# Gated recurrence and highway FFN on one core: zero matmuls in every early wait of TensorE, the diagonal on GpSimd, and a new order of the work

## The chip, the core and the metric

The kernel runs on one core of a Trainium2 chip. TensorE (PE) multiplies matrices into PSUM, a memory of 8 banks; VectorE (DVE), ScalarE (ACT) and GpSimd (POOL) do the rest, and SyncE (SP) issues the loads and stores of the large arrays. The metric is the device time of one execution in microseconds.

## The reference

A recurrence along the sequence, one for each channel, feeds a highway layer. B = 4, S = 6336, D = 256, so the second part has 25344 tokens of 256 channels. All arrays are float32.

```python
sig = 1 / (1 + exp(-f_logit))
f = lower_bound + (1 - lower_bound) * sig
for t in range(S):                       # per batch and channel
    h = f[:, t] * h + (1 - f[:, t]) * x[:, t]
    y[:, t] = h
x = y.reshape(B * S, D)
H = relu(x @ w_h); T = sigmoid(x @ w_t + b_t)
out = T * H + (1 - T) * x
```

## The kernel before

The tokens go through in 22 units: 128, 128, 256 and 512 tokens, four units of 1024, seven double units of 2048 (two loads each), five of 1024, one of 512 and one of 256. Every array is kept channel by channel on the partitions after a transpose on TensorE, in two halves of 128 channels. With u = sigmoid(-f_logit) the kernel computes f = 1 - c*u (c = 1 - lower_bound), scans the product u*x with f into a scaled y, and gets d = max(-c*y, (w_h - I) y) and the gate t = sigmoid(w_t y + b_t) from it. The output is diag(c)*y + d*t, formed by two matmuls that transpose back and add in PSUM.

What runs when is written out by hand in a string, `order`, of one line of tokens after another. Each token calls one small function, and the instructions keep the order of the string on each engine. A token reads "letter, unit.half or unit.chunk.half, colon, place": after the colon stands the SBUF slot or, for work of TensorE, the PSUM bank. A `v` at the end picks the other engine. The letters that the change and the prediction name:

- `l`, `x`: load of f_logit and of x, issued by SP (L279); `wh`, `wt`: loads of the two weights.
- `u`: sigmoid on ACT (L291). `i`: transposes of u (PE, L320). `f`: decay, on ACT (L345) or with `v` on DVE (L343).
- `b`, `B`: half or whole product u*x (L307, L311), on POOL or with `v` on DVE. `p`: transposes of the product (PE, L351 for 128 tokens, L357 beyond). `s`: scan on DVE (L365), whose inputs are f and the transposed product in PSUM.
- `z`, `g`: matmuls of the FFN for the gate and for d (PE, L378 and L156). `t`: gate on ACT (L401). `d`: on DVE (L408). `e`, `E`: half or whole gated product d*t (L422), on POOL or with `v` on DVE.
- `o`: output matmuls (PE, L441 and L442), `c`: copy out of PSUM on ACT (L457) or with `v` on DVE (L455), `w`: store (SP, L464).
- `dg`: the two diagonal matrices diag(c), on POOL (L242) or with `v` on DVE (L240). `cb`: copy of the bias, on DVE or with `v` on ACT. `WI`: w_h - I (POOL, L248). `WH`, `WT`: weights times c (ACT). `pb`, `pc`, `cc`: transposes of the two constants, and c.
- `k*N:bank`: N matmuls of a block of zeros into the second half of a PSUM bank. Nobody reads what they write. The first of a token is recorded at L268, the others through the helper at L156, which long FFN matmuls use too.

The part of the string between the first load and the scan of unit 3 is the place that matters here. `p2.0.1:6 p2.0.0:1`, for example, are the two transposes of unit 2's product, into banks 6 and 1, and `s2.1` and `s2.0` are the scans that read them. The instructions of several engines are recorded one after another, and the tile framework puts a wait wherever a later one touches what an earlier one writes or reads. POOL's two-input operations get one more wait (`shared`): on the last such operation of DVE that was recorded ahead of them.

Of the kernel before, what the change touches and what calls it, by code (L numbers as in the profile page):

```python
# [61 lines left out]
g4.0.0:01 d4.0.0 x6.0:3 l7.0:4 u7.0:16 B6.0:15 p6.0.1:3 s6.1:17 x7.0:5 p6.0.0:6 z5.0.0:45 t5.0.0:19 z5.0.1:01
g5.0.1:45 l8.0:6 e4.0.1 u8.0:25 s6.0 t5.0.1 d5.0.1:9 g5.0.0:23 d5.0.0 l8.1:7 u8.1:14 i7.0.0:7 f7.0v:22 g6.0.0:01
i7.0.1:6 f7.1 e4.0.0 o4.0.1:45 c4.0.1:11 i8.1.1:23 i8.0.1 f8.1:18 x8.0:8 d6.0.0:23 B7.0:8 p7.0.1:6 p7.0.0:7 o4.0.0:45
c4.0.0:13 z6.0.1:01 t6.0.1:21 x8.1:9 s7.0:26 z6.0.0:23 t6.0.0 i8.0.0:45 i8.1.0 f8.0:24 l9.1:1 l9.0:0 g6.0.1:01 B8.0:28
s7.1 z7.0.0:23 t7.0.0:3 g7.0.1:67 B8.1:7 d6.0.1 u9.1:4 E5.0v E6.0 p8.0.1:45 z7.0.1:01 l10.1:2 x9.1:3 x9.0:4 d7.0.1:15
B9.1:6 p8.1.1 t7.0.1 o5.0.1:23 c5.0.1:12 s8.1:16 o5.0.0:67 c5.0.0:8 u9.0:5 p8.0.0:01 p8.1.0 o6.0.0:23 c6.0.0:27
o6.0.1:67 c6.0.1:25 s8.0:22 x10.1:6 u10.1:14 i9.0.0:45 i9.1.0 f9.0:19 l10.0:7 l11.0:5 g7.0.0:23 d7.0.0 B9.0:9
i9.1.1:67 i9.0.1 f9.1:20 x11.1:8 u10.0:28 g8.0.1:01 d8.0.1:7 B10.1:21 w6.0.1 x10.0:9 w2.0.0 g8.1.1:23 d8.1.1:18
p9.1.1:45 p9.0.1 s9.1:17 l11.1:1 E7.0 z8.0.1:01 z8.1.1:67 t8.1.1:23 t8.0.1:4 z8.0.0:23 t8.0.0 i10.1.1:67 i10.0.1  # L70
f10.1:24 p9.1.0:01 p9.0.0 l12.0:0 z8.1.0:23 t8.1.0 i10.1.0:45 w0.0.0 w1.0.0 x13.0:3 x11.0:2 l13.0:4 i10.0.0 f10.0:5
o7.0.0:67 c7.0.0:25 u11.1:6 s9.0:20 g8.1.0:23 u11.0:9 g8.0.0:01 d8.1.0 d8.0.0 g9.1.0:45 d9.1.0:10 z9.0.0:67 t9.0.0:14
l12.1:7 B10.0:3 e8.0.1 g9.1.1:23 d9.1.1 p10.1.0:01 p10.0.0 s10.0:19 z9.1.0:45 t9.1.0:2 o7.0.1:23 c7.0.1:28 E8.1
z9.1.1:67 t9.1.1 e8.0.0 i11.0.1:45 i11.1.1 f11.1:0 p10.0.1:23 p10.1.1 o8.1.1:67 c8.1.1:15 o8.1.0:01 c8.1.0:26 B11.1:23
s10.1:3 E9.1v o8.0.0:45 c8.0.0:21 g9.0.1:67 w4.0.0 o8.0.1:01 c8.0.1:5 x12.1:6 z9.0.1:45 t9.0.1 d9.0.1:4 g10.0.1:23
u12.1:18 w8.1.0 l13.1:9 w3.0.0 g9.0.0:01 d9.0.0 i11.1.0:45 d10.0.1:13 i11.0.0 f11.0:7 g10.1.1:67 d10.1.1:16 g10.0.0:01
d10.0.0 x12.0:1 w6.0.0 B11.0:22 o9.1.0:23 b12.1.0:24 u12.0:2 p11.1.0:45 c9.1.0:6 p11.0.0 s11.0:26 o9.1.1:67 c9.1.1:9
w9.1.1 z10.0.0:01 t10.0.0:1 E9.0 i12.1.1:23 i12.0.1 f12.1:10 z10.1.1:67 t10.1.1:27 p11.0.1:01 p11.1.1 s11.1:22
B12.0:23 o9.0.0:45 c9.0.0:14 o9.0.1:23 c9.0.1:7 z10.0.1:67 t10.0.1 g10.1.0:45 d10.1.0 b12.1.1 u13.1:9 i12.0.0:23
i12.1.0 f12.0:4 u13.0:17 g11.0.1:67 d11.0.1:20 x13.1:5 l14.0:8 w5.0.0 B13.1:2 g11.1.0:01 w8.1.1 w8.0.1 g11.1.1:45  # L80
d11.1.0:0 w8.0.0 d11.1.1 w9.1.0 z11.1.1:67 t11.1.1:18 g11.0.0:23 d11.0.0 z11.1.0:01 t11.1.0 p12.1.1:45 p12.0.1 E10.0v
E11.1 s12.1:8 z11.0.0:23 t11.0.0:15 l21.0:7 l14.1:2 x14.0:0 b13.0.0:5 e11.0.0 z10.1.0:67 z11.0.1:01 t10.1.0 l15.0:1
w9.0.0 x14.1:9 t11.0.1 i13.1.1:23 i13.0.1 f13.1:21 p12.1.0:67 p12.0.0 s12.0:1 o10.0.0:01 c10.0.0:6 o11.1.1:45
c11.1.1:24 w11.1.1 w4.0.1 l16.0:6 e11.0.1v e10.1.1v o10.0.1:23 c10.0.1:23 i13.0.0:01 i13.1.0 f13.0:18 w10.0.1
p13.1.0:45 o11.1.0:23 c11.1.0:10 g12.0.1:67 d12.0.1:13 g12.1.0:01 d12.1.0:9 u14.1:4 g12.0.0:23 d12.0.0 b13.0.1 e10.1.0
u14.0:0 b14.0.1:15 o11.0.0:67 p13.0.0 s13.0:14 c11.0.0:17 o11.0.1:01 c11.0.1:20 z12.0.0:23 t12.0.0:22 i14.1.0:67
i14.0.0 p13.1.1:01 p13.0.1 s13.1:26 f14.0:24 o10.1.0:23 c10.1.0:27 z12.0.1:45 t12.0.1 l17.0:4 B14.1:11 b14.0.0
z12.1.0:67 t12.1.0:2 i14.0.1:23 i14.1.1 f14.1:5 g12.1.1:45 d12.1.1 o10.1.1:67 c10.1.1v:18 g13.1.0:01 d13.1.0:23
l20.0:5 x15.0:2 z13.0.1:23 e12.1.0 g13.0.0:45 u15.0:4 g13.1.1:67 d13.0.0:21 t13.0.1:0 u16.0:3 x16.0:3 z12.1.1:01
t12.1.1 d13.1.1 p14.0.1:23 p14.1.1 s14.1:16 z13.1.1:45 t13.1.1:19 z13.1.0:67 t13.1.0 E12.0 o12.0.0:01 c12.0.0:22  # L90
z13.0.0:45 t13.0.0 p14.0.0:67 w11.0.0 w11.1.0 l18.0:8 w10.1.1 e12.1.1 p14.1.0 i16.0.1:0 f16.1:17 x17.0:9 x19.0:0
x18.0:1 B15.0:10 o12.1.0:12 c12.1.0:2 w12.1.0 w7.0.1 w9.0.1 s14.0:15 o12.1.1:34 c12.1.1:11 i16.0.0:5 i15.0.0:0 f15.0:5
o12.0.1:12 g13.0.1:34 d13.0.1 c12.0.1:18 E13.1 f16.0 u18.0:9 w10.0.0 g14.0.0:67 d14.0.0:1 i15.0.1:0 g14.1.0:12
d14.1.0:8 g14.1.1:34 d14.1.1 g14.0.1:67 d14.0.1 f15.1 p15.0.1:5 s15.1:13 E13.0 u17.0:24 z14.0.0:12 t14.0.0:4 p15.0.0:0
s15.0 z14.1.1:34 B16.0:19 t14.1.1:2 z14.0.1:67 t14.0.1 o13.1.1:12 c13.1.1:10 i17.0.1:3 E14.0v w5.0.1 z14.1.0:45
t14.1.0 w10.1.0 E14.1v b17.0.0:0 w11.0.1 o13.0.0:67 c13.0.0:28 o13.0.1:12 c13.0.1:7 i18.0.1:0 g15.0.0:45 f18.1:6
# [408 lines left out]
```

## Time and profile before

| | |
|---|---|
| median of 3 executions | 209.36 us (209.15 to 209.79) |
| the profiled execution, its own time | 211.39 us |
| its span in the trace | 209.6 us |
| mean granted TensorE clock | 0.995 |
| busy: PE, DVE, ACT, POOL | 191.9, 192.9, 192.7, 171.4 us |
| moved by DMA | 78.68 MB, mean 375 GB/s over the span |

A row of the timeline gives the start (us from the start of the span), the length from there to the end of the last instruction of the group, the engine, the line of the kernel, the operation, out<-in by the program's names, out<-in by shape and type, and the number of instructions. In brackets stands the idle time of the engine just before, and what ended it. A row of groups gives, behind the bar, the busy time in us and the mean of one instruction in ns, and then the idle time before them. A row by stages gives the stage's limits and length, the busy time and instructions of the engine asked for, the granted clock, and the share and rate of the DMA engines.

### The profile page before, as it was taken

The page shows a single profiled execution, that of the slowest core. Times are in us where ns is not written, and L with a number is a line of the kernel's source. Part 1 is how long each engine was busy: PE and PEld are TensorE (multiplying, and loading weights), DVE is VectorE, ACT ScalarE, POOL GpSimd, SP SyncE. Part 2 cuts the span into 40 slices and gives each one's busy share as a digit, 9 for nine tenths or more (in the row PEclk, how much of TensorE's full clock was granted, in tenths as well). Part 3 has the DMA queues.
Part 4 walks back from the last instruction along what each step waited for, and adds up shares of the span by engine and source line. Part 5 has one row for each costly group of instructions (what it writes and reads, how often), then busy time and mean ns, then how long its engine had stood idle before and what let it go on. Part 6 is the DMA issues. An engine that isn't in the chain of part 4 may idle for free.

```text
span 209.6 us, 4643 instructions
## 1 busy us (share of the span) xinstructions
PE 191.9 (92%) x1852; PEld 138.6 (66%) x1877; DVE 192.9 (92%) x138; ACT 192.7 (92%) x193; POOL 171.4 (82%) x72
## 2 busy tenths in 40 slices
PE   7898979799988889999899998999998999999991
PEld 3586846385774647958655967657856886677680
DVE  0667999999999899999999999999999999999981
ACT  4556999999999999999999999999998999998892
POOL 4502489998899999979997978997999599998940
PEclk9999999999999999999999999999999999999998
DMA  5999999999999999799999999999999999664976
GB/s 173 344 429 419 414 421 416 421 419 410 421 420 373 386 428 419 306 277 408 355 344 421 429 417 421 420 418 421 425 413 415 423 411 414 263 245 192 357 263 244
DMA packets 17133, 78.68 MB, mean 375 GB/s; under 512 B 1876, under 2 KB 3160, under 8 KB 11224
## 3 DMA queue, kind: packets, MB, share of 16 engines
q1 hardware_dynamic: 17104, 78.39, 93.7%
q8 instruction: 14, 0.23, 0.4%
q14 instruction: 7, 0.06, 0.1%
q10 hardware_dynamic: 8, 0.00, 0.0%
HBM read 52.43 MB, written 25.95 MB: 374 GB/s over the span
## 4 chain that ended last, share of the span: by engine, by line
PE 32%; ACT 19%; DVE 14%; issue 10%; DMA 5%; POOL 4%; ACTq 0%; DVEq 0%; POOLq 0%
DVE y L365 11%; PE psum L378 10%; ACT t L401 6%; PE psum L156 5%; PE psum L442 5%; PE psum L441 5%; ACT o L457 5%; DMA out_dram<-o 5%; ACT f L345 4%; ACT u L291 3%; PE psum L320 3%; PE psum L357 3%; POOL bv L311 2%; POOL d L422 2%; DVE d L408 2%
## 5 line engine op out<-in xcount | busy, mean ns | idle before, releaser
L365 DVE TENSOR_TENSOR_SCAN y<-f,y,psum 128x1024 bf16<-128x1024 f16 (+7 forms) x42 | 104.4, 2512 | 4.5 <-PE psum L357 3.7
L311 POOL TENSOR_TENSOR bv<-u,x 128x2048 bf16<-128x2048 f16 (+2 forms) x29 | 95.6, 3314 | 8.9 <-issue 3.9
L422 POOL TENSOR_TENSOR d<-d,t 128x1024 bf16<-128x1024 bf16 (+3 forms) x28 | 72.8, 2618 | 18.7 <-ACT t L401 11.1
L378 PE MATMUL psum<-y,w_sb 128*128 128x512 bf16 (+2 forms) x242 | 78.6, 363 | 4.6 <-DVE y L365 2.0
L408 DVE SCALAR_TENSOR_TENSOR d<-y,ncc,psum 128x1024 bf16<-128x1024 bf16 (+3 forms) x62 | 62.9, 1056 | 1.2 <-PE psum L156 0.5
L401 ACT ACTIVATE t<-psum,bt 128x1024 bf16<-128x1024 f32 (+3 forms) x62 | 57.9, 983 | 5.8 <-PE psum L378 2.2
L156 PE MATMUL psum<-y,w_sb 128*128 128x512 bf16 x149 | 56.4, 379 | 0.7 <-DVE y L365 0.6
L345 ACT ACTIVATE f<-psum,ncc 128x1024 f16<-128x1024 f16 (+4 forms) x40 | 52.1, 1323 | 2.6 <-PE psum L320 2.6
L291 ACT ACTIVATE u<-l 128x2048 f16<-128x2048 f32 (+3 forms) x29 | 49.3, 1720 | 2.1 <-DMA l<-in_f_logit_dram 2.1
L457 ACT COPY o<-psum 128x1024 f32<-128x1024 f32 (+2 forms) x55 | 48.5, 926 | 1.9 <-PE psum L442 1.8
L442 PE MATMUL psum<-ident_b,d 128*128 128x128 bf16 x396 | 48.7, 219 | 1.3 <-POOL d L422 1.1
L441 PE MATMUL psum<-diag,y 128*128 128x128 f16 x396 | 48.9, 219 | 0.2
L442 PEld LDWEIGHTS <-d 128*128 128x128 bf16 x396 | 43.5, 112 | 4.6 <-POOL d L422 1.9
L441 PEld LDWEIGHTS <-y 128*128 128x128 bf16 x396 | 43.6, 112 | 1.8
L378 PEld LDWEIGHTS <-w_sb 128*128 128x128 f16 x248 | 23.5, 99 | 20.3 <-DVE y L365 2.1
L320 PE MATMUL psum<-ident_h,u 128*128 128x128 f16 x396 | 29.3, 221 | 2.7 <-ACT t L401 1.7
L320 PEld LDWEIGHTS <-u 128*128 128x128 f16 x396 | 25.3, 99 | 8.4 <-issue 3.1
L357 PE MATMUL psum<-ident_f,bv 128*128 128x128 f32 x196 | 28.0, 276 | 0.7 <-POOL bv L311 0.7
L156 PEld LDWEIGHTS <-w_sb 128*128 128x128 f16 x168 | 16.4, 97 | 18.1 <-issue 3.7
L357 PEld LDWEIGHTS psum<-ident_f,bv 128*128 128x128 f32 x196 | 22.3, 142 | 5.8 <-POOL bv L311 1.7
L422 DVE TENSOR_TENSOR d<-d,t 128x2048 bf16<-128x2048 bf16 (+3 forms) x12 | 10.5, 891 | 0.4 <-ACT t L401 0.3
L156 PE MATMUL psum<-zeros 128*128 128x256 bf16 x55 | 9.8, 322 | 0.0
(36 smaller groups left out, 45.0 us busy)
## 6 DMA issues: line engine op xcount, KB each, us to landing
l<-in_f_logit_dram SPq DMA_DIRECT2D x23, 1024.0 KB, 15.9
x<-in_x_dram SPq DMA_DIRECT2D x23, 1024.0 KB, 15.9
out_dram<-o SPq DMA_DIRECT2D x43, 512.0 KB, 9.0
out_dram<-o SPq DMA_DIRECT2D x12, 256.0 KB, 2.4
l<-in_f_logit_dram SPq DMA_DIRECT2D x2, 512.0 KB, 10.1
...
```

Of the source, the lines that this page charges most:

```text
L156: return pe.add_instruction(mybir.InstMatmult(name=nc.get_next_instruction_name(), start_tensor_calc=start, stop_tensor_calc=stop, tile_si ...
L311: shared(pin(e.tensor_mul(st[n]["bv", s][:, a:c].rearrange("p k d j -> p k j d"), st[n]["u", s][:, 2 * a:2 * c].rearrange("p (k j) d -> p ...
L320: pin(nc.tensor.transpose(uT[:, j * P:(j + 1) * P], st[n]["u", s][:, j, h * P:(h + 1) * P], ident_h))
L345: pin(nc.scalar.activation(to, of, AF.Identity, scale=ncc[:, h:h + 1], bias=1.0))
L365: pin(nc.vector.tensor_tensor_scan(y[:, c:e], st[n]["f", h][:, c:e], data, 0.0 if fresh else carry[h], op0=ALU.mult, op1=ALU.add))
L378: pin(nc.tensor.matmul(p.part(a, e), w, data, start=ki == 0, stop=ki == NH - 1))
L401: pin(nc.scalar.activation(half(n, q, "t", m), z, AF.Sigmoid, bias=bt[:, m:m + 1]))
L408: pin(nc.vector.scalar_tensor_tensor(half(n, q, "d", m), y, ncc[:, m:m + 1], g, op0=ALU.mult, op1=ALU.max))
L422: shared(pin(e.tensor_mul(d, d, t)), not eng)
L441: pin(nc.tensor.matmul(o, st[n]["y", h][:, whole], diag[:, h], start=True, stop=False))
L442: pin(nc.tensor.matmul(o, half(n, q, "d", h)[:, cols], ident_b, start=False, stop=True))
L457: pin(nc.scalar.copy(to, op))
```

## The change

Only the string changes, in all its lines; the functions, the units, the shapes and the arithmetic stay.

- Zeros: 72 before the middle of the program instead of 65, in more and other places. Before, in order: 2, 4, 2, 12, 8, 4, 5 and 23 in bank 7, 3 in bank 5, 2 in bank 6. After: 1, 2, 4, 2, 1, 3, 14, 3, 2, 5, 1, 1, 1, 24 and 2 in bank 7, 6 in bank 6.
- `dgv` becomes `dg`: the diagonal moves from DVE to POOL, and later in the string. `cbv` becomes `cb`: the bias is copied by DVE instead of ACT.
- Decays: f0.1, f1.0, f1.1 and f2.0 go to DVE (f0.0 stays, f2.1 moves to ACT); f7.1 instead of f7.0 on DVE; f21.0 from DVE to ACT.
- Gated products: E0.0 and the second half of E2.0 move from DVE to POOL; E20.0 is whole on DVE instead of half; E18.0 instead of E19.0 is on DVE.
- First loads: x0, l0, l1, l2, x1, x2, wh, wt instead of l1, l0, x0, l2, x1, wh, x2, wt.
- PSUM banks: p2.0.1 and p2.0.0 go to banks 5 and 7 (6 and 1 before), p3.0.1 and p3.0.0 to 7 and 0 (3 and 1 before), g1.0.1 to 7 (6 before).
- The rest of the work stands in another order, with other slots and banks.

```diff
-i2.0.0:5 f2.0 p1.0.1:4 WI WH cbv x2.0:5 wt WT b2.0.0:10 k*12:7 p2.0.1:6 p2.0.0:1 g0.0.0:7 dgv s1.1 s2.1:11 s2.0
...
-B3.0v:20 z0.0.0:0 z2.0.0:4 t2.0.0 d2.0.0 e2.0.0 E1.0 t0.0.0 e2.0.1v k*5:7 p3.0.1:3 s3.1:21 l4.0:8 u4.0:22 p3.0.0:1
-s3.0 k*23:7 z3.0.0:5 t3.0.0:23 i4.0.1:2 f4.1:24 E0.0v x4.0:9 B4.0v:25 g3.0.0:6 z3.0.1:7 t3.0.1 d3.0.0:26 e3.0.0
...
+i2.0.1:4 f2.1:9 x2.0:5 b2.0.0:10 i2.0.0:1 f2.0v k*3:7 p2.0.1:5 p2.0.0:7 p1.0.1:4 wh WI s1.1 WH k*14:7 g1.0.0:6
+g0.0.0:0 g0.0.1:3 s2.0:11 wt WT k*3:7 z1.0.1:2 z0.0.1:1 s2.1 z1.0.0:4 g1.0.1:7 k*2:7 z2.0.1:5 d0.0.1:12 l3.0:6 u3.0:13
+z2.0.0:3 t1.0.1:14 t1.0.0 k*5:7 g2.0.0:2 k*1:7 i3.0.1:4 t2.0.0:15 t2.0.1 d1.0.0:16 t0.0.1:17 f3.1:18 g2.0.1:6 z0.0.0:3
+t0.0.0 k*1:7 i3.0.0:5 f3.0 dg d1.0.1 d0.0.0 x3.0:7 b3.0.1v:19 l4.0:8 u4.0:20 b3.0.0v k*1:7 p3.0.1:7 p3.0.0:0 E0.0
+d2.0.0:21 k*24:7 i4.0.1:1 f4.1:22 x4.0:9 d2.0.1 s3.1:23 E2.0 s3.0 z3.0.0:2 z3.0.1:4 B4.0v:24 g3.0.0:3 d3.0.0:25
...
```

In the built program the first place is TensorE around the transposes of unit 2's product (`bv_167` before, `bv_157` after; `psum_61` is all of PSUM; the scan reads what the L357 rows write). Before:

```order
L156 LDWEIGHTS zeros_62
L156 MATMUL psum_61<-zeros_62 128x256
L357 MATMUL psum_61<-ident_f_71,bv_167 128x128 [waits DVE_49,Pool_49]
L357 MATMUL psum_61<-ident_f_71,bv_167 128x128
L378 LDWEIGHTS w_sb_96 [waits Activation_49]
L378 MATMUL psum_61<-y_143,w_sb_96 128x128
```

After:

```order
L156 LDWEIGHTS zeros_62
L156 MATMUL psum_61<-zeros_62 128x256
L357 MATMUL psum_61<-ident_f_71,bv_157 128x128 [waits Pool_49]
L357 MATMUL psum_61<-ident_f_71,bv_157 128x128
L351 LDWEIGHTS bv_143
L351 MATMUL psum_61<-ident_b_76,bv_143 128x128 [waits Activation_49]
L268 LDWEIGHTS zeros_62
L268 MATMUL psum_61<-zeros_62 128x256
```

Before, the twelve zeros of `k*12:7` stand ahead of the transposes, and an FFN matmul follows them. Now three zeros stand ahead; behind the transposes come that of unit 1's second half (L351, which waits for ACT) and the fourteen zeros of `k*14:7`.

The second place is TensorE around the transposes of unit 3's product (`bv_253` and `bv_264`). Before:

```order
L156 LDWEIGHTS zeros_62
L156 MATMUL psum_61<-zeros_62 128x256
L357 MATMUL psum_61<-ident_f_71,bv_253 128x128 [waits DVE_49]
L357 MATMUL psum_61<-ident_f_71,bv_253 128x128 x3
L268 LDWEIGHTS zeros_62
L268 MATMUL psum_61<-zeros_62 128x256
```

After:

```order
L320 LDWEIGHTS u_219
L320 MATMUL psum_61<-ident_h_66,u_219 128x128
L268 LDWEIGHTS zeros_62
L268 MATMUL psum_61<-zeros_62 128x256 [waits DVE_49]
L357 MATMUL psum_61<-ident_f_71,bv_264 128x128 [waits DVE_49]
L357 MATMUL psum_61<-ident_f_71,bv_264 128x128 x3
L268 LDWEIGHTS zeros_62
L268 MATMUL psum_61<-zeros_62 128x256
```

A block of zeros follows the transposes in both (23 before, 24 now). Before, that block stands behind `s3.1` and `s3.0` in the string, and writes to bank 7, from which no scan of unit 3 reads; now it stands ahead of `s3.1` and writes to the bank of p3.0.1.

The third place is DVE from the scans of unit 2 (`y_188` before, `y_194` after) to those of unit 3 (`y_272`, `y_316`); `d_197`, `d_201`, `d_240` before and `d_215`, `d_241`, `d_277` after belong to units 0, 1 and 2. Before:

```order
L365 SCALAR_TENSOR_TENSOR y_188<-f_136,y_145,psum_61 128x256 [waits PE_49,Activation_49]
L408 SCALAR_TENSOR_TENSOR d_197<-y_143,ncc_93,psum_61 128x128 [waits PE_49]
L408 SCALAR_TENSOR_TENSOR d_201<-y_145,ncc_93,psum_61 128x128 [waits PE_49]
L408 SCALAR_TENSOR_TENSOR d_197<-y_143,ncc_93,psum_61 128x128 [waits PE_49]
L408 SCALAR_TENSOR_TENSOR d_201<-y_145,ncc_93,psum_61 128x128 [waits PE_49]
L408 SCALAR_TENSOR_TENSOR d_240<-y_188,ncc_93,psum_61 128x256 [waits DVE_49]
L311 TENSOR_TENSOR bv_253<-u_195,x_251 128x2x2x256 [waits DMAHW3_49,Activation_49]
L408 SCALAR_TENSOR_TENSOR d_240<-y_188,ncc_93,psum_61 128x256 [waits DVE_49,PE_49]
L422 TENSOR_TENSOR d_240<-d_240,t_224 128x256 [waits DVE_49,Activation_49]
L365 SCALAR_TENSOR_TENSOR y_272<-f_237,y_188,psum_61 128x512 [waits PE_49,Activation_49]
```

After:

```order
L365 SCALAR_TENSOR_TENSOR y_194<-f_153,y_148,psum_61 128x256 [waits DVE_49]
L408 SCALAR_TENSOR_TENSOR d_215<-y_135,ncc_93,psum_61 128x128 [waits PE_49]
L408 SCALAR_TENSOR_TENSOR d_241<-y_148,ncc_93,psum_61 128x128
L408 SCALAR_TENSOR_TENSOR d_241<-y_148,ncc_93,psum_61 128x128 [waits PE_49]
L408 SCALAR_TENSOR_TENSOR d_215<-y_135,ncc_93,psum_61 128x128
L311 TENSOR_TENSOR bv_264<-u_219,x_262 128x2x256 [waits DMAHW3_49,Activation_49]
L311 TENSOR_TENSOR bv_264<-u_219,x_262 128x2x256
L408 SCALAR_TENSOR_TENSOR d_277<-y_194,ncc_93,psum_61 128x256 [waits DVE_49,Activation_49]
L408 SCALAR_TENSOR_TENSOR d_277<-y_194,ncc_93,psum_61 128x256 [waits DVE_49]
L365 SCALAR_TENSOR_TENSOR y_316<-f_245,y_194,psum_61 128x512 [waits PE_49,Activation_49]
```

The product of unit 3 (L311) stands behind all four d of units 0 and 1 in both; its two halves are instructions of their own now, both d of unit 2 come behind them, and the half gated product (L422) has left DVE here.

More of the change, by code (lines that the diff above doesn't have):

```diff
@@ L62 @@
[L62 to L96, printed above, removed]
```

81 lines of the change are left out of this document (57 added, 24 removed).

## The prediction

> **What bounds the kernel now.** I read the page's busy shares first, then the busy time of the vector engine (DVE) by stages, then the first 30 us of each engine in order of time.
>
> ```profile
> span 209.6 us, 4643 instructions
> PE 191.9 (92%) x1852; PEld 138.6 (66%) x1877; DVE 192.9 (92%) x138; ACT 192.7 (92%) x193; POOL 171.4 (82%) x72
> ```
>
> Three engines are busy for 92% of the span, so the average does not say which one is late. The stages do (start:end, length, DVE busy and instructions, granted clock, DMA share, GB/s):
>
> ```profile
> 0.00:4.50 4.50, 0.27 (x1) 1.00 0.47 152
> 4.50:18.00 13.50, 8.23 (x20) 1.00 0.99 388
> 18.00:205.60 187.60, 184.43 (x117) 1.00 0.96 384
> 205.60:209.60 4.00, 0.00 (x0) 0.75 0.55 202
> ```
>
> From 18.0 to 205.6 us DVE rests for 187.60 - 184.43 = 3.17 us in all. Whatever moves the moment at which DVE starts to run without a break therefore moves the end, less what of these 3.17 us can be given back. That moment is the scan of unit 3, s3.1, at 18.01:
>
> ```profile
> 5.22 0.28 DVE L343 TENSOR_SCALAR f<-psum,ncc 128x128 f16<-128x128 f16 x1 [0.42 <-PE psum L156]
> 8.47 1.06 DVE L240 TENSOR_SCALAR diag<-ident_h,cc 128x128 f16<-128x128 f16 x2
> 9.46 0.47 DVE L365 TENSOR_TENSOR_SCAN y<-f,y,psum 128x128 bf16<-128x128 f16 x1
> 11.69 1.39 DVE L365 TENSOR_TENSOR_SCAN y<-f,y,psum 128x256 bf16<-128x256 f16 x2 [1.76 <-PE psum L357]
> 12.99 0.58 DVE L408 SCALAR_TENSOR_TENSOR d<-y,ncc,psum 128x128 bf16<-128x128 bf16 x2
> 13.75 0.35 DVE L408 SCALAR_TENSOR_TENSOR d<-y,ncc,psum 128x128 bf16<-128x128 bf16 x1 [0.18 <-PE psum L156]
> 14.31 0.74 DVE L408 SCALAR_TENSOR_TENSOR d<-y,ncc,psum 128x128 bf16<-128x128 bf16 x2 [0.20 <-PE psum L378]
> 14.96 1.30 DVE L311 TENSOR_TENSOR bv<-u,x 128x1024 bf16<-128x1024 f16 x1
> 16.15 0.48 DVE L408 SCALAR_TENSOR_TENSOR d<-y,ncc,psum 128x256 bf16<-128x256 bf16 x1
> 18.01 2.45 DVE L365 TENSOR_TENSOR_SCAN y<-f,y,psum 128x512 bf16<-128x512 f16 x2 [1.18 <-PE psum L357]
> 20.38 0.27 DVE L422 TENSOR_TENSOR d<-d,t 128x256 bf16<-128x256 bf16 x1
> 20.56 2.47 DVE L311 TENSOR_TENSOR bv<-u,x 128x2048 bf16<-128x2048 f16 x1
> ```
>
> The brackets tell what the old order loses: 1.76 us before s2 and 1.18 us before s3, both on TensorE's transposes of the products (L357). Two smaller brackets matter more for the new order. At 5.22 f0.0, and at 13.75 d0.0.0, wait for L156 as a zero matmul, an instruction whose result nobody reads. Here is TensorE at the same time:
>
> ```profile
> 8.88 2.55 PE L156 MATMUL psum<-zeros 128*128 128x256 bf16 x11
> 11.23 0.63 PE L357 MATMUL psum<-ident_f,bv 128*128 128x128 f32 x2
> 12.29 0.42 PE L268 MATMUL psum<-zeros 128*128 128x256 bf16 x1
> 12.51 1.21 PE L156 MATMUL psum<-zeros 128*128 128x256 bf16 x7
> 14.65 0.49 PE L156 MATMUL psum<-zeros 128*128 128x256 bf16 x3
> 16.98 0.27 PE L268 MATMUL psum<-zeros 128*128 128x256 bf16 x1 [0.95 <-ACT t L401]
> 17.52 0.60 PE L357 MATMUL psum<-ident_f,bv 128*128 128x128 f32 x4
> 18.07 2.13 PE L156 MATMUL psum<-zeros 128*128 128x256 bf16 x18
> ```
>
> The eight zeros of 12.29 and 12.51 end at 13.72, and d0.0.0 starts at 13.75. Its operand g0.0.0 lies in bank 7, whose other half those zeros write, and in the built program its wait counts up to the last of them. So a reader of a PSUM bank that stands behind a block of zeros of the same bank, in the order's text, waits for the whole block. At 16.98 the reverse is seen: the zeros of bank 7 wait 0.95 us for the reader t0.0.1.
>
> These rows also give the price of a zero. From the first start to the last it is (2.55 - 0.42)/10 = 0.213 us early on, and (2.13 - 0.27)/17 = 0.109 us later; the block at 12.51 is where the pace doubles.
>
> **The change, part by part.** The diagonal: the DVE row at 8.47 loses its 1.06 us. GpSimd does it now, in a gap that these rows show:
>
> ```profile
> 6.80 0.87 POOL L248 TENSOR_TENSOR w_raw<-w_raw,ident_f 128x128 f32<-128x128 f32 x2 [0.58 <-DMA w_raw<-in_moe_w_h_dram]
> 8.16 1.17 POOL L311 TENSOR_TENSOR bv<-u,x 128x512 bf16<-128x512 f16 x1 [0.49 <-DMA x<-in_x_dram]
> 17.37 1.30 POOL L422 TENSOR_TENSOR d<-d,t 128x256 bf16<-128x256 bf16 x2 [8.04 <-ACT t L401]
> ```
>
> The 8.04 us of idle hide it; without them it could cost what GpSimd needs for 128x128 of floats, 0.87/2 us each by its subtraction of the identity (the row at 6.80), 0.9 us. I take zero for GpSimd. On DVE the gain also counts nothing, since DVE has to wait for TensorE right behind it.
>
> The fill ahead of s2. Before, 12 zeros stood ahead of the transposes p2, which therefore came at 11.23, although the product was ready at 8.16 + 1.17 = 9.33. Now 3 zeros stand there, so p2 can run near 9.4, which alone would give s2 some 1.8 us. But p2.0.0 goes to bank 7, and k*14:7 stands between it and s2.0. The 14 zeros start behind p1.0.1, which waits for f2.1; from f2's row of 8.81 and x2.0's earlier place in the load queue I put that at 9.9. At the early pace they last 14 x 0.213 = 2.98 us (to 12.9), at the late pace 14 x 0.109 = 1.53 us (to 11.4). I take 12.4, nearer to the early pace, because the row at 8.88 shows it until past 11 and the change to the fast one falls into the row at 12.51. Then s2.0 starts at 12.6 instead of 11.69, and both scans end at 14.0 (1.39 us).
>
> ```profile
> 8.81 0.47 ACT L345 ACTIVATE f<-psum,ncc 128x256 f16<-128x256 f16 x1 [0.89 <-PE psum L320]
> 10.83 1.04 ACT L291 ACTIVATE u<-l 128x1024 f16<-128x1024 f32 x1
> 14.04 0.99 ACT L401 ACTIVATE t<-psum,bt 128x128 bf16<-128x128 f32 x3 [2.17 <-PE psum L378]
> 15.40 1.26 ACT L345 ACTIVATE f<-psum,ncc 128x512 f16<-128x512 f16 x2 [0.37 <-PE psum L320]
> ```
>
> and, by shape, the gates of unit 2 (instructions, busy us, mean ns, idle before):
>
> ```profile
> L401 ACT ACTIVATE t<-psum,bt 128x256 bf16<-128x256 f32 x4 | 2.0, 494 | 0.0
> ```
>
> The next hold. d0.0.1 and d1.0.0 follow (0.58 us, to 14.6). d1.0.1 reads bank 7, and the last zero of that bank ahead of it stands behind z0.0.0, which waits for t2.0.0. The first gate t1.0.1 can start once three zeros behind s2.0 and z1.0.1 are through, at 13.3 + 0.33 + 0.4 = 14.0, as before (14.04). Two gates of 0.33 (0.99/3) and t2.0.0 of 0.49, which first waits for z2.0.0, bring ScalarE to 15.5. TensorE still has i3.0.1, g2.0.1 and z0.0.0 in front, so the zero is through at about 16.3 and d1.0.1 runs at 16.5. DVE rests for 1.9 us, where the old order had 0.18 and 0.20.
>
> Then d1.0.1 and d0.0.0 (0.7 us, to 17.2), the two halves of unit 3's product (1.30 us together as in the row at 14.96, to 18.5), d2.0.0 and d2.0.1 (0.9 us, to 19.4).
>
> The large fill. p3.0.1 goes to bank 7 now (bank 3 before) and k*24:7 stands between it and s3.1. TensorE transposes from 18.6 for about 0.45 us (four starts of 0.11 us, row 17.52), then come 24 x 0.109 = 2.6 us of zeros: s3.1 starts at 18.6 + 0.45 + 2.6 + 0.2 = 21.9. In the old order the row at 18.07 ran beside s3. Idle on DVE: 2.5 us. f3.1 and f3.0 (0.63 us each, row at 15.40), which follow two more gates, end at 17 and 18 and are in time.
>
> Sum at s3.1: 21.9 - 18.01 = +3.9 us. Everything on DVE, ScalarE's f4 and t3, and GpSimd's next work hang on s3 and are as late.
>
> Work behind it. DVE loses E0.0 (0.27, row 20.38, now on GpSimd) and f21.0, and has E20.0 whole instead of half; the forms by shape:
>
> ```profile
> L422 DVE TENSOR_TENSOR d<-d,t 128x1024 bf16<-128x1024 bf16 x3 | 1.9, 673 | 0.0
> L343 DVE TENSOR_SCALAR f<-psum,ncc 128x256 f16<-128x256 f16 x2 | 1.0, 480 | 1.3 <-PE psum L320 1.3
> L422 DVE TENSOR_TENSOR d<-d,t 128x512 bf16<-128x512 bf16 x2 | 0.9, 426 | 0.4 <-ACT t L401 0.3
> ```
>
> That is -0.27 - 0.48 + (0.67 - 0.43) = -0.5 us. The scans, the d's and the copies on DVE stay the same in kind and number. Of the 3.17 us that DVE rests behind 18.0, a late DVE gives back those in which it waits for something that is not late itself, such as a transfer. Nearly all engines are late by the same amount here, so I take 0.6 us; the ends are 0 and 3.17. The tail behind DVE's last work (205.6 to 209.6) is alike in both orders: last copies, three stores. Sum: +3.9 - 0.5 - 0.6 = +2.8 us on the span of 209.6, 212.4. The profiled execution's own time is 211.39, 1.8 us around its span; the median of the runs shown is 209.36, 2.0 us below it. I lay the difference on the median: 212.2.
>
> The other moves in the order (about sixty lines) leave instructions, shapes and banks alike in kind. I cost them at nothing, and give them a bound of 1.2 us either way from the 3.17 us that can at most be saved there.
>
> **The clock of TensorE.** The rows of TensorE show half its later pace until the block at 12.51, where eleven zeros stand in the row at 8.88 alone. The Trainium skill, "TensorE: Matmul & The Clock Gate", section "What's actually happening", says that a busy window of about 3.4 us releases the full clock, from whatever the windows' phase is. The granted clock in the stages above is 1.00 throughout and does not show it, while the durations do agree with a factor of two. By the skill a better filled start would be at full pace earlier. What that would do here follows from the rows alone: 14 zeros end at 11.4 instead of 12.4, and the chain behind them is 1.0 us earlier. TensorE still has a gap in the new order ahead of k*2:7, which waits for s0.0 in its bank, so I keep this as a rival.
>
> **Rivals.**
> Full pace at 10 us: the sum becomes 212.2 - 1.0 = 211.2.
> The middle gives it back: if DVE's 3.17 us of idle all but vanish (3.0), the time is 209.36 + 3.4 - 3.0 = 209.8. For it: so little idle is left that small moves in sixty lines could close it. Against it: TensorE and ScalarE, for which DVE waits there, are late too.
> The middle gets worse: transfers and buffers were placed for an earlier DVE; 1.2 us more and nothing given back make about 214.0.
> The zeros do not hold DVE (faster): if the readers of bank 7 wait only for their own transposes, s2.0 runs at 10.6, d1.0.1 at 13.8, p3 is ready at 16.7 and s3.1 runs at about 16.9, 1.1 us earlier than now; with 0.5 us less work the time is 207.8. It decides at s3.1: below 18.0 the change wins. Against it stand the two L156 brackets.
>
> **How the numbers follow.** The forecast (211.6 to 213.4) has 0.51, early full pace 0.14, the worse middle 0.12, the middle that gives back 0.11, the faster case 0.12. A difference of 0.3% (0.63 us: 208.7 to 210.0) is about what a measurement can tell from no change. Slower: 0.51 + 0.14 + 0.12 + half of 0.11 = 0.82; same: the other half, 0.06; faster 0.12. The range leaves out the faster case, a quarter of the giving back and the far end (a third) of the worse middle, 0.19 in all: 209.6 to 214.4.
>
> **What the profile after would show.** DVE's scan of 128x256 released by a zero matmul (L156) after some 2 us of idle; the second pair of d's idle until a zero (L268) at about 16.5; the scan of 128x512 at about 21.9, released by L156, with about 2.5 us of idle; the stage from 18 to the end with hardly less DVE work than before. I am wrong if s3.1 starts before 18, or if DVE's idle behind it falls below 1 us.

## The result and the profile after

The changed kernel takes 214.95 us (median of 4, 214.21 to 215.98) against 209.37 us of the kernel before in the same comparison: a ratio of 1.0267, interval 1.0212 to 1.0322, slower. In a later comparison, of six executions, it took 213.91 us against 210.15 us: 1.0176, interval 1.0124 to 1.0227. The ratios, here and below, are formed from the executions in the faster of two states in which each kernel runs, so they are not exactly those of the medians. The profiled execution took 214.31 us with a span of 212.1 us.

The page's first lines:

```profile
span 212.1 us, 4659 instructions
PE 193.1 (91%) x1859; PEld 139.6 (66%) x1884; DVE 191.4 (90%) x139; ACT 191.9 (90%) x190; POOL 172.0 (81%) x71
```

DVE by stages (start:end, length, busy time and instructions, granted clock, DMA share, GB/s):

```profile
4.50:18.00 13.50, 6.97 (x21) 0.87 1.02 402
18.00:205.60 187.60, 181.91 (x115) 0.99 0.94 377
205.60:212.10 6.50, 2.21 (x5) 1.00 0.76 282
```

The whole program has 1.5 us less work for DVE (192.9 before), and still ends later. DVE in order of time:

```profile
12.21 1.39 DVE L365 TENSOR_TENSOR_SCAN y<-f,y,psum 128x256 bf16<-128x256 f16 x2 [1.97 <-PE psum L156]
13.51 0.58 DVE L408 SCALAR_TENSOR_TENSOR d<-y,ncc,psum 128x128 bf16<-128x128 bf16 x2
16.18 0.61 DVE L408 SCALAR_TENSOR_TENSOR d<-y,ncc,psum 128x128 bf16<-128x128 bf16 x2 [2.08 <-PE psum L268]
16.70 1.34 DVE L311 TENSOR_TENSOR bv<-u,x 128x512 bf16<-128x512 f16 x2
17.93 0.86 DVE L408 SCALAR_TENSOR_TENSOR d<-y,ncc,psum 128x256 bf16<-128x256 bf16 x2
21.48 2.45 DVE L365 TENSOR_TENSOR_SCAN y<-f,y,psum 128x512 bf16<-128x512 f16 x2 [2.69 <-PE psum L156]
```

Against the old order, where s3 started at 18.01 us after 1.18 us of rest, three pauses now stand ahead of it: 1.97 us before s2, released by the zeros (L156; the old order rested 1.76 us there, for the transposes themselves), 2.08 us before d1.0.1, released by a zero (L268), and 2.69 us before s3.1, again by L156. TensorE shows what they wait for:

```profile
8.99 0.63 PE L357 MATMUL psum<-ident_f,bv 128*128 128x128 f32 x2
9.52 0.42 PE L268 MATMUL psum<-zeros 128*128 128x256 bf16 x1
9.73 2.44 PE L156 MATMUL psum<-zeros 128*128 128x256 bf16 x13
18.09 0.66 PE L357 MATMUL psum<-ident_f,bv 128*128 128x128 f32 x4 [1.24 <-DVE bv L311]
18.59 0.27 PE L268 MATMUL psum<-zeros 128*128 128x256 bf16 x1
18.70 2.67 PE L156 MATMUL psum<-zeros 128*128 128x256 bf16 x23
23.98 2.48 PE L378 MATMUL psum<-y,w_sb 128*128 128x512 bf16 x7 [2.17 <-DVE y L365]
```

The transposes p2 run at 8.99 us and are through by 9.62. s2.0, which reads one of them, starts at 12.21, just behind the last of the 14 zeros (9.73 + 2.44 = 12.17). The transposes p3 are through by 18.75; the 24 zeros behind them end at 21.37, and s3.1 starts at 21.48. The zeros write the other half of the same bank and nobody reads them.

The Trainium skill, "PSUM — Partial Sum Buffer", section "PSUM bank collisions raise a hardware error", says that accesses of two engines must be kept apart by bank and quadrant of partitions, not by address, and that the chip itself doesn't stall. The traces agree that the hold goes by the bank (the halves are disjoint, and the same zeros in another bank hold nobody: a_k24 below); here it is in the program's waits.

GpSimd (POOL) makes the diagonal in its gap:

```profile
8.71 1.19 POOL L242 TENSOR_SCALAR diag<-ident_h,cc 128x128 f16<-128x128 f16 x2
18.18 1.83 POOL L422 TENSOR_TENSOR d<-d,t 128x256 bf16<-128x256 bf16 x2 [8.29 <-DVE bv L311]
```

It takes 1.19 us, and 8.29 us of idle follow.

### The profile page after: what moved, and what is told of

Read it like the earlier page. It is cut to its first block, busy times and chain, and to the rows that moved or that the text cites. A ratio compares the mean times of both kernels' runs of the same rounds, so it can differ in the third digit from the quotient of the medians.

```text
span 212.1 us, 4659 instructions
## 1 busy us (share of the span) xinstructions
PE 193.1 (91%) x1859; PEld 139.6 (66%) x1884; DVE 191.4 (90%) x139; ACT 191.9 (90%) x190; POOL 172.0 (81%) x71
## 4 chain that ended last, share of the span: by engine, by line
PE 55%; ACT 18%; DVE 9%; issue 9%; DMA 4%; POOL 2%; SPq 1%; ACTq 0%; DVEq 0%
PE psum L378 18%; PE psum L156 12%; PE psum L441 6%; PE psum L442 6%; PE psum L357 6%; PE psum L320 5%; ACT t L401 5%; ACT o L457 5%; ACT f L345 5%; DVE y L365 4%; ACT u L291 4%; DVE d L408 3%; DMA out_dram<-o 3%; POOL d L422 2%; DMA l<-in_f_logit_dram 1%
## 5 line engine op out<-in xcount | busy, mean ns | idle before, releaser
L311 POOL TENSOR_TENSOR bv<-u,x 128x2048 bf16<-128x2048 f16 (+2 forms) x27 | 95.3, 3545 | 8.5 <-DVE d L422 5.4
L422 POOL TENSOR_TENSOR d<-d,t 128x2048 bf16<-128x2048 bf16 (+3 forms) x27 | 72.8, 2713 | 20.6 <-DVE bv L311 14.6
L345 ACT ACTIVATE f<-psum,ncc 128x1024 f16<-128x1024 f16 (+3 forms) x38 | 51.4, 1380 | 7.8 <-PE psum L320 7.6
L156 PE MATMUL psum<-y,w_sb 128*128 128x512 bf16 x150 | 56.8, 379 | 0.3 <-DVE y L365 0.2
L357 PE MATMUL psum<-ident_f,bv 128*128 128x128 f32 x196 | 28.8, 279 | 2.9 <-POOL bv L311 1.4
L357 PEld LDWEIGHTS psum<-ident_f,bv 128*128 128x128 f32 x196 | 23.0, 143 | 8.8 <-DVE bv L311 1.8
L156 PEld LDWEIGHTS <-w_sb 128*128 128x128 f16 x168 | 16.4, 97 | 17.3 <-issue 2.9
L365 DVE TENSOR_TENSOR_SCAN y<-f,psum 128x128 bf16<-128x128 f16 (+3 forms) x8 | 9.6, 1201 | 0.1
L422 DVE TENSOR_TENSOR d<-d,t 128x1024 bf16<-128x1024 bf16 (+2 forms) x11 | 9.1, 853 | 0.2
```

The lines of the kernel that those rows point to most:

```text
L156: return pe.add_instruction(mybir.InstMatmult(name=nc.get_next_instruction_name(), start_tensor_calc=start, stop_tensor_calc=stop, tile_si ...
L311: shared(pin(e.tensor_mul(st[n]["bv", s][:, a:c].rearrange("p k d j -> p k j d"), st[n]["u", s][:, 2 * a:2 * c].rearrange("p (k j) d -> p ...
L345: pin(nc.scalar.activation(to, of, AF.Identity, scale=ncc[:, h:h + 1], bias=1.0))
L357: pin(nc.tensor.transpose(words[:, k:k + g * (P - 1) + 1:g], pair, ident_f))
L365: pin(nc.vector.tensor_tensor_scan(y[:, c:e], st[n]["f", h][:, c:e], data, 0.0 if fresh else carry[h], op0=ALU.mult, op1=ALU.add))
L422: shared(pin(e.tensor_mul(d, d, t)), not eng)
```

## The experiments

In the new order the end of the span lies a nearly constant time behind the start of s3.1. Under "ratio" stands the time against the kernel before on the same chip, with its interval; s3.1 and the span are those of the profiled execution, whose rows stand below; that is one execution of several, and where it lies at the edge of them the text says so.

| kernel | time us | ratio | s3.1 | span | span - s3.1 |
|---|---|---|---|---|---|
| before (first trace) | 209.36 | | 18.01 | 209.6 | 191.6 |
| changed | 214.95 | 1.0267 (1.0212 to 1.0322) | 21.48 | 212.1 | 190.6 |
| changed, again (after_2) | 213.91 | 1.0176 (1.0124 to 1.0227) | 20.93 | 211.8 | 190.9 |
| 24 zeros moved (a_k24) | 209.60 | 1.0010 (0.9962 to 1.0058) | 16.40 | 206.7 | 190.3 |
| early zeros moved (a_k14d1) | 210.38 | 1.0014 (0.9981 to 1.0048) | 17.47 | 208.7 | 191.2 |
| all moved (a_all) | 208.72 | 0.9957 (0.9905 to 1.0008) | 17.73 | 208.5 | 190.8 |
| no zeros (a_noz) | 207.64 | 0.9889 (0.9802 to 0.9976) | 14.53 | 205.6 | 191.1 |
| 12 instead of 24 (a_h12) | 213.15 | 1.0113 (1.0056 to 1.0171) | 21.26 | 212.6 | 191.3 |
| few zeros (a_few) | 207.53 | 0.9886 (0.9850 to 0.9921) | 15.02 | 205.7 | 190.7 |
| few, diagonal on DVE (a_few_dgv) | 207.66 | 0.9915 (0.9887 to 0.9943) | 14.23 | 205.5 | 191.3 |
| before with a hold (b_hold) | 214.83 | 1.0199 (1.0087 to 1.0312) | 20.60 | 213.4 | 192.8 |
| before, few zeros (b_few) | 209.07 | 0.9982 (0.9949 to 1.0016) | 14.72 | 206.5 | 191.8 |
| before, diagonal on POOL (b_dg) | 210.73 | 1.0023 (0.9988 to 1.0057) | 15.53 | 207.7 | 192.2 |

In the new order s3.1 starts anywhere from 14.2 to 21.5 us and the end follows 190.3 to 191.3 us behind it; in the old order it is 191.6 to 192.8 us, and 193.1 in one more trace (below). That is the prediction's first claim, that this start sets the end.

**The 24 zeros in another bank (a_k24).**

```diff
-d2.0.0:21 k*24:7 i4.0.1:1 ...
+d2.0.0:21 k*24:5 i4.0.1:1 ...
```

> The changed kernel with its 24 zeros behind p3 moved from bank 7 to bank 5, which no scan of unit 3 reads; nothing else. Theory 1 (a reader of a PSUM bank is held by the zeros of that bank recorded ahead of it): s3.1 starts at about 19.0 us instead of 21.5, released by the transposes (L357), and the time falls by about 2.3 us. Theory 2 (more zeros take TensorE's clock down, and its slower matmuls cost the time): the 24 zeros still run, s3.1 may move but the end stays within 0.7 us of the changed kernel. Theory 3 (the loss is in the order of the later units): within 0.7 us too, and what s3 gains is waited for later.

DVE and TensorE of this kernel:

```profile
9.91 1.39 DVE L365 TENSOR_TENSOR_SCAN y<-f,y,psum 128x256 bf16<-128x256 f16 x2 [1.05 <-PE psum L156]
13.88 0.61 DVE L408 SCALAR_TENSOR_TENSOR d<-y,ncc,psum 128x128 bf16<-128x128 bf16 x2 [2.08 <-PE psum L268]
16.40 2.45 DVE L365 TENSOR_TENSOR_SCAN y<-f,y,psum 128x512 bf16<-128x512 f16 x2
8.29 1.58 PE L156 MATMUL psum<-zeros 128*128 128x256 bf16 x13
16.39 2.67 PE L156 MATMUL psum<-zeros 128*128 128x256 bf16 x23
19.35 1.89 PE L378 MATMUL psum<-y,w_sb 128*128 128x512 bf16 x7
```

The same 24 zeros run beside s3 now (16.39), and s3.1 has no bracket left: the hold of 2.69 us is gone. The ratio falls from 1.0176 (after_2, on another chip) to 1.0010, some 3.5 us, with the two intervals 2 to 5 us. That rules out theories 2 and 3 (at most 0.7 us), and does not rule out the 2.3 us that were expected. The trace shows s3.1 earlier than expected (16.40, not 19.0), but it is that of the fastest of ten executions, and 2.3 us of the difference stand ahead of s2 already (9.91 against 12.21): the first loads came 0.7 us sooner (the first sigmoid starts at 3.77 instead of 4.47), p2 runs at 7.84 instead of 8.99, and the 13 zeros took 1.58 us, not 2.44. The holds before s2 (1.05 us here) and d1.0.1 (2.08 us) remain.

**The early zeros in other banks (a_k14d1).**

```diff
-... s1.1 WH k*14:7 g1.0.0:6
+... s1.1 WH k*14:1 g1.0.0:6
-... g1.0.1:7 k*2:7 z2.0.1:5 ... k*5:7 g2.0.0:2 k*1:7 i3.0.1:4 ... t0.0.0 k*1:7 i3.0.0:5 ...
+... g1.0.1:7 k*2:1 z2.0.1:5 ... k*5:1 g2.0.0:2 k*1:1 i3.0.1:4 ... t0.0.0 k*1:2 i3.0.0:5 ...
```

> The changed kernel with the 14 zeros in bank 1 and those between g1.0.1 and d1.0.1 in banks 1 and 2; the 24 zeros stay in bank 7 ahead of s3.1. Theory 1: s2 runs at about 10.3 us, but TensorE carries the same zeros, so p3 comes at about 17 and s3.1 at 20 to 20.5, held by L156 for 2.5 to 3 us; the time falls by about 1 us against the changed kernel, far less than a_k24 fell. If the early holds were the cost, it falls by more than 2.5 us.

DVE:

```profile
9.02 1.76 DVE L365 TENSOR_TENSOR_SCAN y<-f,y,psum 128x128 bf16<-128x128 f16 x3
11.82 0.61 DVE L408 SCALAR_TENSOR_TENSOR d<-y,ncc,psum 128x128 bf16<-128x128 bf16 x2 [0.17 <-PE psum L378]
17.47 2.45 DVE L365 TENSOR_TENSOR_SCAN y<-f,y,psum 128x512 bf16<-128x512 f16 x2 [2.53 <-PE psum L156]
```

s2 follows s1.1 without a rest (three scans in the row at 9.02), the pause before d1.0.1 shrinks from 2.08 to 0.17 us, and s3.1 is still held, by 2.53 us. The expectation of only 1 us was wrong: 3.4 us came back (1.0176 to 1.0014; 2.1 to 4.7 us with the two intervals). I had taken TensorE for late by the zeros themselves; in fact p3 of the changed kernel waits 1.24 us for DVE's product (row at 18.09), and here it runs at 14.15 us without that wait. So the early hold was on the path. Not all of the gain in this trace is the hold: the 13 zeros took 1.58 us here, against 2.19 in after_2.

**All of them in other banks (a_all)** has both edits.

> The changed kernel with all three holds taken away: the 24 zeros in bank 5, the 14 zeros behind p2 in bank 1, the zeros between g1.0.1 and d1.0.1 in banks 1 and 2; their numbers and places in the order stay. Theory 1: s2.0 at about 10.3 us (12.2 in the changed kernel), d1.0.1 at about 14 (16.2), s3.1 at about 17 (21.5); the time falls by 3.5 to 4.5 us against the changed kernel. Theory 2: at most 1 us. Theory 3: s3.1 moves, the end moves by less than 2 us.

DVE, and TensorE's 13 zeros behind p2:

```profile
10.31 1.76 DVE L365 TENSOR_TENSOR_SCAN y<-f,y,psum 128x128 bf16<-128x128 f16 x3 [0.69 <-PE psum L351]
17.73 2.44 DVE L365 TENSOR_TENSOR_SCAN y<-f,y,psum 128x512 bf16<-128x512 f16 x2
10.28 2.98 PE L156 MATMUL psum<-zeros 128*128 128x256 bf16 x13
```

4.6 us came back against the changed kernel (1.0176 to 0.9957), about as forecast; but the two edits don't add up (3.5 + 3.4). The trace is that of the slowest of ten executions (210.69 us; the others took 207.74 to 209.37). What is left in it is the zeros' own length: 13 of them took 2.98 us, and the d of units 0 and 1 waited 1.85 us for FFN matmuls behind them.

**No zeros (a_noz)** drops every `k` token.

> The changed kernel without any of its 72 zeros in units 0 to 5 (the six of the very start stay). Theory 1: no reader is held; s3.1 at 16 to 18.5 us, the time 3 to 5 us below the changed kernel, whatever TensorE's pace. Theory 2: the granted clock shows no dips below 0.95 in the first 30 us, and the time falls as much. A rule that TensorE must be kept busy to run at full pace: the early matmuls of 128x128 take twice as long (a start every 0.11 us instead of 0.055), s3.1 is later than in the kernel with the zeros in other banks.

DVE, and TensorE's FFN matmuls of the first units:

```profile
14.53 2.45 DVE L365 TENSOR_TENSOR_SCAN y<-f,y,psum 128x512 bf16<-128x512 f16 x2 [0.56 <-PE psum L357]
9.18 3.42 PE L378 MATMUL psum<-y,w_sb 128*128 128x128 bf16 x20 [0.15 <-ACT w_sb L255]
```

The 20 matmuls take 3.42 us, 0.17 us each, about half the pace that they have in a_k24 (eight in 0.61 us), and the granted clock is 0.50 from 9 to 12 us. Yet s3.1 starts 6.9 us before that of the changed kernel, earlier than expected (16 to 18.5), and the time falls by 6.0 us (1.0176 to 0.9889), more than the 3 to 5 us expected. The rule in the expectation is half right here: the early matmuls are slower, but s3.1 is not later than in a_all (17.73). The second theory, that TensorE's lower clock is what costs the time, falls here: the clock is lower and the kernel is faster, 0.9889 against the kernel before.

**The kernel before with such a hold (b_hold).**

```diff
-... p3.0.1:3 s3.1:21 l4.0:8 u4.0:22 p3.0.0:1
-s3.0 k*23:7 ...
+... p3.0.1:7 l4.0:8 u4.0:22 p3.0.0:1 k*23:7
+s3.1:21 s3.0 ...
```

> The kernel before with p3.0.1 in bank 7 instead of 3 and its 23 zeros recorded ahead of s3.1 instead of behind s3.0; all else as before. Theory 1: s3.1 starts at 20 to 20.7 us instead of 18.0, released by L156, and the time rises by about 2 us against the kernel before. Theories 2 and 3: the zeros run at the same place on TensorE as before, and the time stays within 0.6 us of the kernel before.

DVE:

```profile
20.60 2.45 DVE L365 TENSOR_TENSOR_SCAN y<-f,y,psum 128x512 bf16<-128x512 f16 x2 [3.91 <-PE psum L156]
```

With a rest of 3.91 us ahead of s3.1 the old order loses 2.0%, 4.2 us (1.8 to 6.6 us by the interval), from one bank number and the place of the zeros and the scans. About 2 us were expected, which the interval still holds, and the trace shows 2.6 us: its s2 starts at 11.68 as in the first trace of the kernel before (11.69), and s3.1 at 20.60 instead of 18.01.

**Half of the 24 zeros (a_h12)** has `k*12:7` in place of `k*24:7`.

> The changed kernel with 12 zeros instead of 24 in bank 7 ahead of s3.1. Theory 1: s3.1 waits for 12 zeros less, 1.3 us at the pace of 0.109 us, 2.6 us where they run at 0.213, and the time falls by as much (1.3 to 2.6 us). If the hold has a cost that does not depend on the number of zeros (TensorE's rest behind them and a lower pace after it), it falls by less than 0.7 us.

DVE:

```profile
21.26 2.45 DVE L365 TENSOR_TENSOR_SCAN y<-f,y,psum 128x512 bf16<-128x512 f16 x2 [1.39 <-PE psum L156]
```

The rest before s3.1 is 1.39 us instead of 2.69: 12 zeros less take 1.30 us off it, and the ratio falls by 0.63%, 1.3 us. The intervals of the two ratios overlap, so it is the bracket that shows it: the cost goes by the number of zeros, 0.108 us each. (This execution was late already at s2; only the bracket is compared.)

**Few zeros (a_few)** leaves out 14, 3, 2, 5, 1, 1 and 1 of bank 7 and the 6 of bank 6, and has 12 in bank 5 instead of the 24.

> The changed kernel without the zeros from p2 to p3 (14, 3, 2, 5, 1, 1, 1, 1) and without the 6 in bank 6, with 12 in bank 5 instead of 24 in bank 7; the early ones stay. Theory 1: s3.1 at 13.5 to 15 us, as in a_noz (14.5), and a time 1 to 2% below the kernel before. If the zeros that were left out had kept TensorE's pace, s3.1 comes later than in a_noz, at 15 to 17 us.

DVE:

```profile
15.02 2.45 DVE L365 TENSOR_TENSOR_SCAN y<-f,y,psum 128x512 bf16<-128x512 f16 x2 [0.33 <-PE psum L357]
```

It beats both kernels: 207.53 us, 0.9886, with all six times between 207.35 and 207.81. With most of its zeros out of the way, the new kernel is about 2.4 us (0.0114 of 210) faster than the old one with its zeros.

**The kernel before with few zeros (b_few)** leaves out its 12, 8, 4 and 5.

> The kernel before without its zeros from p2 to p3 (12, 8, 4 and 5); the first 8, the 23 behind s3 and the later 5 stay. If the zeros' own length ahead of p2 and of the FFN matmuls is what the new order without them gains, p2 runs at about 9.4 us, s3 starts at 15 to 16.5, and the time falls by 1 to 3 us, to that of a_few. If the gain lies in the new order (loads, decays on DVE, the diagonal), the time falls by less than 0.7 us.

DVE:

```profile
9.54 1.38 DVE L365 TENSOR_TENSOR_SCAN y<-f,y,psum 128x256 bf16<-128x256 f16 x2 [1.06 <-PE psum L357]
14.72 2.45 DVE L365 TENSOR_TENSOR_SCAN y<-f,y,psum 128x512 bf16<-128x512 f16 x2 [0.55 <-PE psum L357]
```

The trace has s3.1 at 14.72 and a span of 206.5, but that is the shortest of 12 executions (206.5 to 209.0), and the ratio is 0.9982 with an interval over 1. A gain of 1 to 3 us isn't confirmed. The intervals of a_few (up to 0.9921) and b_few (from 0.9949) don't touch. So the zeros' length alone is not what a_few gains; the rest of the new order has a part in it, and which of its moves it is the runs don't show.

**The diagonal.** b_dg has `dg` for `dgv` in the kernel before, a_few_dgv `dgv` for `dg` in a_few.

> The kernel before with the diagonal on POOL instead of DVE, at its place; nothing else. By the prediction DVE waits for TensorE right behind it, so nothing is won: s2 and s3 start as before, the time is within 0.5 us of the kernel before. If two engines at one port slow each other there, DVE's rows of 8 to 12 us get longer or shorter by a visible part and the time moves by more.

> a_few with the diagonal on DVE instead of POOL, at its place in the order (ahead of d1.0.1). DVE works there nearly without a break, so its two instructions (0.53 us each) lie on the path but for the 0.66 us that it waits for a gate: s3 is 0.4 to 1.1 us later than in a_few, the time 0.4 to 1 us longer. If the diagonal's engine doesn't matter here either, within 0.3 us.

DVE and POOL of b_dg, then DVE of a_few_dgv:

```profile
15.53 2.45 DVE L365 TENSOR_TENSOR_SCAN y<-f,y,psum 128x512 bf16<-128x512 f16 x2 [1.10 <-PE psum L357]
9.41 1.19 POOL L242 TENSOR_SCALAR diag<-ident_h,cc 128x128 f16<-128x128 f16 x2
11.38 0.41 DVE L240 TENSOR_SCALAR diag<-ident_h,cc 128x128 f16<-128x128 f16 x2
14.23 2.44 DVE L365 TENSOR_TENSOR_SCAN y<-f,y,psum 128x512 bf16<-128x512 f16 x2
```

Neither ratio differs from its base beyond the intervals; the 0.4 to 1 us expected for a_few_dgv is thus neither confirmed nor ruled out, though its s3.1 came earlier than that of a_few, not later. On DVE the diagonal takes 0.41 us here, on POOL 1.19 us. What it costs on DVE depends on POOL: see the last section.

**What differs between executions.** The same two kernels, traced again.

> The changed kernel once more, beside the others of this batch on one chip, for the size of the loss and for a second trace. Theory 1 with the rest of the order as fast as before: the end stays 190.6 us (within 0.5) behind the start of s3, in this execution too, and the loss against the kernel before is 3 to 6 us, as s3 starts 3 to 6 us later. Theory 2: the pace of the 14 and 24 zeros (0.109 or 0.213 us each) differs between executions, so s3 lies anywhere from 20.5 to 24 us, and the times spread by more than those of a_k24 did.

> The changed kernel, a third trace. If the difference between executions is the pace of the early zeros, the span is 190.9 us (within 0.5) behind s3.1's start, and s3.1 moves with the time that the 14 and the 24 zeros take: near 20 us where all run at 0.109 us, near 21.5 where most of the 14 run at 0.213. If the difference arises behind s3, the distance from s3 to the end varies by more than 1 us.

> The changed kernel, a fourth trace: 190.9 us (within 0.5) from the start of s3.1 to the end if the early pace decides, more variation than 1 us if something behind s3 does.

> The kernel before once more, for a second trace of it. The theory on the size: its first trace (span 209.6) ran its 12 zeros ahead of p2 at 0.213 us each, and in other executions these zeros run at 0.109 us. If this trace shows that pace, s2 and s3 start 1.2 to 2.8 us earlier and the span is 206.5 to 208; if it shows the slow pace, s3 starts at about 18 and the span is 209 to 210. Against it: a span under 208 with s3 at 18, or over 209 with s3 before 17.

> The kernel before, a third trace. If the pace of the early zeros makes the difference between executions, the span is 191.7 us (within 0.7) behind s3.1's start, s3.1 lies near 15.5 where the 12 zeros ahead of p2 run at 0.109 us and at 16.8 to 18 where they run at 0.213. If not, s3 is near one value and the distance to the end varies.

> The kernel before, a fourth trace: 191.7 us (within 0.7) from the start of s3.1 to the end if the early pace decides, more variation if something behind s3 does.

s3.1 in after_2, after_3 and after_4, then in before_3 and before_4 (before_2 stands below):

```profile
20.93 2.45 DVE L365 TENSOR_TENSOR_SCAN y<-f,y,psum 128x512 bf16<-128x512 f16 x2 [2.69 <-PE psum L156]
20.91 2.45 DVE L365 TENSOR_TENSOR_SCAN y<-f,y,psum 128x512 bf16<-128x512 f16 x2 [2.69 <-PE psum L156]
22.61 2.45 DVE L365 TENSOR_TENSOR_SCAN y<-f,y,psum 128x512 bf16<-128x512 f16 x2 [2.69 <-PE psum L156]
17.96 2.45 DVE L365 TENSOR_TENSOR_SCAN y<-f,y,psum 128x512 bf16<-128x512 f16 x2 [1.19 <-PE psum L357]
16.08 2.45 DVE L365 TENSOR_TENSOR_SCAN y<-f,y,psum 128x512 bf16<-128x512 f16 x2 [1.09 <-PE psum L357]
```

With spans of 211.8, 211.7 and 213.2 us, the end of the changed kernel is 190.9, 190.8 and 190.6 us behind: the start of s3.1 makes all the difference between its executions. From s2 to s3.1 all four traces need the same 9.26 or 9.27 us. From p2 to s2, where the 14 zeros stand, they need 2.97 to 3.35 us. The larger part of the difference lies ahead of p2, which runs at 8.99, 8.69, 8.54 and 10.00 us; here are p2 and the 13 zeros of after_3, then of after_4:

```profile
8.54 0.64 PE L357 MATMUL psum<-ident_f,bv 128*128 128x128 f32 x2
9.28 2.32 PE L156 MATMUL psum<-zeros 128*128 128x256 bf16 x13
10.00 0.63 PE L357 MATMUL psum<-ident_f,bv 128*128 128x128 f32 x2
10.75 2.56 PE L156 MATMUL psum<-zeros 128*128 128x256 bf16 x13
```

Ahead of p2 the first loads come at different times (the first sigmoid starts at 3.90 us in after_3, at 4.68 in after_4), and three earlier zeros took 0.49 us in the one and 0.85 in the other. So the pace of the 14 zeros, which the expectations put first, is the smaller part.

In the kernel before the spans are 208.2, 209.4 and 209.2 us, with 191.4, 191.4 and 193.1 us behind 16.84, 17.96 and 16.08; in the last, which lies outside the 191.7 us (within 0.7) that was expected, DVE rested more between 120 and 180 us (2.2 us, against 0.6 in the first trace) and gave back most of its early start. before_2 fits neither of its two cases: its 11 zeros took 2.50 us, the slow pace, and s3.1 still starts at 16.84. TensorE's 11 zeros ahead of p2 in before_3, then in before_4 with p2:

```profile
8.90 2.55 PE L156 MATMUL psum<-zeros 128*128 128x256 bf16 x11
7.85 1.36 PE L156 MATMUL psum<-zeros 128*128 128x256 bf16 x11
10.04 0.44 PE L357 MATMUL psum<-ident_f,bv 128*128 128x128 f32 x2 [0.83 <-POOL bv L311]
```

They take 2.55 us in the one and 1.36 us in the other, where p2 then waits for the product itself. The granted clock shows 1.00 in both. The Trainium skill, "TensorE: Matmul & The Clock Gate", section "What's actually happening", says that the gate's windows run free of the kernel's start, so that the moment of full pace varies between runs; the traces agree: the same 13 zeros took 1.58, 2.19, 2.32, 2.44, 2.56 or 2.98 us in different executions of the new order. a_noz had none and lost nothing by it.

## Why the prediction was right, and where it was wrong

**Right: direction, place and mechanism.** By its steps, forecast and then measured in the first trace: p2 near 9.4 (8.99); s2.0 at 12.6 (12.21); d1.0.1 at 16.5 after 1.9 us of rest (16.18 after 2.08); p3 at 18.6 (18.09); s3.1 at 21.9 after 2.5 us of rest (21.48 after 2.69). The sum for the span was 212.4; it is 212.1. That these agree so well is in part luck, because s3.1 differs between executions by up to 1.7 us, and because the part behind s3.1 came out right by parts that are not as forecast. It is 1.0 us shorter (191.6 to 190.6), where -0.5 us of DVE work and -0.6 us of idle were forecast. DVE's work behind s3.1 fell by 1.1 us (184.4 to 183.3), its idle rose by 0.6 us (3.1 to 3.7), and the tail behind its last instruction, put down as alike, fell by 0.5 us (4.1 to 3.5). So nothing of the idle was given back. Here are DVE's rows from s3.1 to its last instruction, before and after:

```profile
18.01:205.53 187.52, 184.42 (x117) 1.00 0.96 384
21.48:208.56 187.08, 183.34 (x116) 0.99 0.94 376
```

The diagonal was rightly costed at nothing within the interval of b_dg, though POOL needs 1.19 us for it, above my upper end of 0.9. (The granted clock is not 1.00 in all the stages shown, as the prediction says: the last has 0.75.)

**Wrong: the time, 212.2 us forecast with 214.4 as the end, 214.95 measured.** The step that failed is the last of the sum, where I said "I lay the difference on the median". The difference was worked out from one execution of the kernel before, which took 211.39 us; the median of the others, 209.36 us, is 2.03 us lower. Laid on the execution that it was worked out from, +2.8 us gives 214.2, and the profiled execution of the changed kernel took 214.31 us. Laid on the median it loses the 2.03 us, as if the executions behind the median had started s3.1 at 18.01 too. There is no trace of them, but the later comparisons have spans of 206.3 to 210.3 us for the same kernel, with medians of 208.2 to 208.5, so the traced span of 209.6 is a long one; and s3.1 at 18.01 is the latest of four traces (16.08, 16.84, 17.96, 18.01; mean 17.2), while the changed kernel has a mean of 21.5 (20.91 to 22.61). The term "+3.9 at s3.1" is therefore +4.3 between means, the part behind it -1.2 (191.9 and 190.7), together +3.1 us of span. The later comparison has +3.8 us of time (213.91 against 210.15), 1.0 us more than the forecast's +2.8; 0.3 us of it lies outside the span (2.1 us there in the changed kernel, 1.8 in the kernel before).

**Open:** the first comparison's +5.6 us. Its kernel before was 0.7 to 0.9 us faster than in the later comparisons (medians 210.05 to 210.27), its changed kernel 1.0 us slower; it has four executions of each, and its interval for the ratio and that of the repeat just touch (1.0212 and 1.0227). Two of the changed kernel's executions had spans of 213.4 and 214.1 us; there is a trace of neither. By the constant distance their s3.1 would have started at 22.7 and 23.4 us; the latest on a trace is 22.61 (after_4). Why the executions of one kernel differ this much at their start stays open.

**The rivals.** The zeros do hold DVE: the rival "zeros do not hold DVE" is out by the three brackets and by a_k24 and a_k14d1. The middle gave back none of DVE's idle, and it did not get worse: the distance from s3.1 to the end is 1.0 us shorter. So "the middle gets worse" is out as well, although its 214.0 lies nearest to the measured time. Full pace at 10 us was not seen in any of the four traces of the changed kernel (its 13 zeros took 2.19 to 2.56 us), only in variants.
